# Attention batches of four tiles across head groups, with the engine of the k and q evacuations chosen by position

## The chip, the cores and the metric

One NeuronCore of one Trainium2 chip runs the whole program. The metric is the device time of one execution in microseconds (us), median of several. The profile's span is that time without about 1.8 us around it. PE is TensorE's matmul stream, PEld its weight loads, DVE is VectorE, ACT is ScalarE, POOL is GpSimd, SP the engine that issues the DMAs; SPq and the like are the issuing side of an engine. TensorE writes into PSUM, a memory of eight banks; an *evacuation* is the copy by which ScalarE or VectorE takes a finished result out of a bank, so that the bank can be written again.

## The reference

Two attention blocks read the same x (2048 rows, 1024 columns, 32 heads of 32) and are mixed by a gate. A is linear attention; B, in which the change lies, lets each query see 8 keys at distances 0, 2, ..., 14.

```python
x = A_x
g = sigmoid((x * gate_w).sum(-1, keepdims=True))
a = A_ref(x, A_wqkv, A_wo)     # phi(q) (phi(k)^T v) / (phi(q) sum phi(k)), then @ wo
b = B_ref(x, B_wqkv, B_wo)     # softmax over 8 keys at distance 0, 2, ... 14, then @ wo
return g * a + (1 - g) * b
```

## The kernel before

Rows are sorted by parity, so that the 8 keys of a query are neighbours. A *tile* is one head group (4 heads) and 112 queries (128 at the start of a parity) against 128 keys; a head group has 18 tiles, 8 head groups have 144. A *score batch* computes the scores of some tiles into four PSUM banks, one per head; ScalarE takes the exp, VectorE multiplies by the band mask; a *value batch* then multiplies by V. The batches of head group c-1 are strewn between the 64 wide matmuls (8 groups of 8) that project k and q of head group c. Positions count these matmuls. The code is shortened and put together from the kernel; the kernel itself has every line.

```python
CUTS4 = (0, 4, 8, 12, 15, 18)        # 5 batches per head group: 4, 4, 4, 3, 3 tiles
CUTS3 = (0, 3, 6, 9, 12, 15, 18)     # the last head group: 6 batches of 3
# k and q projection, one group of 8 matmuls:
    nc.tensor.matmul(st["pj"][:], lhsT=W[...], rhs=xT[:, kt, cols], ...)   # 128x512, two PSUM banks in turn
    if kt == KT - 1:
        if which == 0: nc.scalar.copy(out=kqt[:, 0, cols], in_=st["pj"][:])          # k: ScalarE
        else:          nc.vector.tensor_copy(out=kqt[:, 1, cols], in_=st["pj"][:])   # q: VectorE
# scores(g), one score batch:
    s4 = ps_s.tile([P, 4, 512], F32, ...)                    # four banks, not doubled
    for q0, w, k0 in tiles:
        for i in range(4):                                   # four heads: four 32-row tiles of the array
            r = slice(32 * i, 32 * i + 32)
            nc.tensor.matmul(s4[:, i, o:o + w], lhsT=kqt[r, 0, k0:k0 + P], rhs=kqt[r, 1, q0:q0 + w], ...)
        o += w
    for h in range(2):                                       # exp and mask, two heads at a time
        nc.scalar.activation(out=ptv[:, hs], in_=s4[:, hs, 0:W_], func=ACT.Exp, scale=SCALE)
        nc.vector.tensor_tensor(out=ptv[:, hs], in0=ptv[:, hs], in1=mask..., op=ALU.mult)
# pv(g), one value batch, 17 matmuls later: 128-row matmuls of 33 columns (V and a column of ones),
# then reciprocal and product on VectorE, then a DMA transpose (all cut)
ev.append((first + step * g, scores)); ev.append((first + step * g + lag, pv))   # step = 64 / batches
```

Of the kernel before, what the change touches and what calls it, by code (L numbers as in the profile page):

```python
# [7 lines left out]
ACT = mybir.ActivationFunctionType  # L8
ALU = mybir.AluOpType
BF16 = mybir.dt.bfloat16  # L10
F32 = mybir.dt.float32
PE = mybir.EngineType.PE
DVE = mybir.EngineType.DVE
P = 128
# [14 lines left out]
def interleave(units, events):  # L29

    events = sorted(events, key=lambda e: e[0])
    for i, unit in enumerate(units):
        while events and events[0][0] <= i:
            events.pop(0)[1]()
        unit()
    for _, fn in events:
        fn()
# [3 lines left out]
def kernel(  # L41
# [11 lines left out]
    nc = tc.nc  # L53
    S, D = A_x.shape[1:]
# [9 lines left out]
    Dh = D // H  # L64
# [1 line left out]
    NB = S // P  # L66
    SCALE = float(Dh) ** -0.5
    QT = query_tiles()
    CUTS4 = (0, 4, 8, 12, 15, 18)
    CUTS3 = (0, 3, 6, 9, 12, 15, 18)  # L70

    nc.scalar.preload_act_table_set("natural_log_exp_and_others")

    consts = ctx.enter_context(tc.tile_pool(name="consts", bufs=1))
# [48 lines left out]
    def band(dst, lead):  # L123
        nc.gpsimd.memset(dst, 1.0)
        for base, sign in ((lead, 1), (7 - lead, -1)):
            nc.gpsimd.affine_select(out=dst, in_=dst, compare_op=ALU.is_ge, fill=0.0, base=base,
                                    pattern=[[sign, dst.shape[1]]], channel_multiplier=-sign)

    mask = consts.tile([P, 128 + 5 * 112], BF16, name="mask")
    band(mask[:, 112:240], 0)  # L130
    for o in (0, 240, 352, 464, 576):
        band(mask[:, o:o + 112], 16)
    gdot = consts.tile([P, NB], F32, name="gdot")
    ratio = consts.tile([P, NB], F32, name="ratio")
# [13 lines left out]
    with tc.manual_schedule(engines={PE}):  # L148
# [172 lines left out]
        with ExitStack() as s2:  # L321
# [10 lines left out]
            def kq_units(c, kqt):  # L332
                def mm(b, which, kt, st):
                    W = (WkB, WqB)[which]
                    cols = slice(b * 512, (b + 1) * 512)
                    if kt == 0:
                        st["pj"] = ps_pj.tile([P, 512], F32, name="kq_ps", tag="pj")
                    nc.tensor.matmul(st["pj"][:], lhsT=W[c // 4][:, kt, (c % 4) * P:(c % 4 + 1) * P],  # L338
                                     rhs=xT[:, kt, cols], start=(kt == 0), stop=(kt == KT - 1))
                    if kt == KT - 1:  # L340
                        if which == 0:
                            nc.scalar.copy(out=kqt[:, 0, cols], in_=st["pj"][:])
                        else:
                            nc.vector.tensor_copy(out=kqt[:, 1, cols], in_=st["pj"][:])  # L344
                for b in range(4):
                    for which in range(2):
                        st = {}
                        for kt in range(KT):
                            yield lambda b=b, which=which, kt=kt, st=st: mm(b, which, kt, st)

            count = [0]

            def attention_events(c, kqt, cuts, first, lag):
                GROUPS = [QT[a:b] for a, b in zip(cuts, cuts[1:])]
                state = [dict() for _ in GROUPS]
                per_bank = 2 if cuts is CUTS4 else 3

                def scores(g):
                    tiles, st = GROUPS[g], state[g]
                    W_ = sum(w for _, w, _ in tiles)  # L360
                    s4 = ps_s.tile([P, 4, 512], F32, name="s4", tag="s")
                    o = 0
                    for q0, w, k0 in tiles:
                        for i in range(4):
                            r = slice(32 * i, 32 * i + 32)
                            nc.tensor.matmul(s4[:, i, o:o + w], lhsT=kqt[r, 0, k0:k0 + P],
                                             rhs=kqt[r, 1, q0:q0 + w], start=True, stop=True)
                        o += w
                    pt = PT[count[0] % 2]
                    count[0] += 1  # L370
                    ptv = pt[:, 0:4 * W_].rearrange("p (i s) -> p i s", i=4)
                    m0 = 112 if tiles[0][1] == 128 else 0 if tiles[1][1] == 128 else 240
                    for h in range(2):
                        hs = slice(2 * h, 2 * h + 2)
                        nc.scalar.activation(out=ptv[:, hs], in_=s4[:, hs, 0:W_], func=ACT.Exp, scale=SCALE)  # L375
                        m = mask[:, m0:m0 + W_]
                        nc.vector.tensor_tensor(out=ptv[:, hs], in0=ptv[:, hs],  # L377
                                                in1=m[:, None, :].broadcast_to([P, 2, W_]), op=ALU.mult)
                    st["pt"], st["W"] = pt, W_

                def pv(g):
                    tiles, st = GROUPS[g], state[g]
                    pt, W_, n = st["pt"], st["W"], len(tiles)
                    Ob = small.tile([P, 4, 4, Dh], BF16, name="Ob", tag="Ob", bufs=4)
                    oB = []
                    for b in range((n + per_bank - 1) // per_bank):
                        bank = ps_o.tile([P, 512], F32, name=f"oB{b}", tag=f"o{b}")
                        m = min(per_bank, n - per_bank * b)
                        oB.append((b * per_bank, m, bank[:, 0:m * 4 * (Dh + 1)].rearrange("p (t i e) -> p t i e", t=m, i=4)))
                    for t0, m, o_ in oB:  # L390
                        for i in range(4):
                            o = sum(w for _, w, _ in tiles[:t0])
                            for tt in range(t0, t0 + m):
                                nc.tensor.matmul(o_[:, tt - t0, i, :], lhsT=pt[:, i * W_ + o:i * W_ + o + P],
                                                 rhs=V[:, cuts[g] + tt, c * 4 + i, :], start=True, stop=True)
                                o += tiles[tt][1]
                    for t0, m, o_ in oB:
                        rd = small.tile([P, 3, 4, 1], F32, name="rd", tag="rd")
                        nc.vector.reciprocal(out=rd[:, 0:m], in_=o_[:, :, :, Dh:Dh + 1])
                        nc.vector.tensor_tensor(out=Ob[:, t0:t0 + m], in0=o_[:, :, :, 0:Dh],  # L400
                                                in1=rd[:, 0:m].broadcast_to([P, m, 4, Dh]), op=ALU.mult)
                    t0 = 0
                    while t0 < n:
                        q0, w, _ = tiles[t0]
                        m = 1
                        while t0 + m < n and tiles[t0 + m][1] == w and tiles[t0 + m][0] == q0 + m * w:
                            m += 1
                        nc.sync.dma_start_transpose(
                            out=OBT[:, c, q0:q0 + m * w].rearrange("p (t s) -> p t s", t=m),
                            in_=Ob[0:w, t0:t0 + m].rearrange("p t i e -> p (t i e)"))  # L410
                        t0 += m

                ev = []
                step = 64 / len(GROUPS)
                for g in range(len(GROUPS)):
                    ev.append((first + step * g, lambda g=g: scores(g)))
                    ev.append((first + step * g + lag, lambda g=g: pv(g)))
                return ev

            carry = []  # L420
            prev = None
            for c in range(KT):
                kqt = kq.tile([P, 2, S], BF16, name="kqt", tag="kq")
                ev = carry + (attention_events(c - 1, prev, CUTS4, 3, 17) if c else [])
                interleave(list(kq_units(c, kqt)), [e for e in ev if e[0] < 64])
                carry = [(p - 64, f) for p, f in ev if p >= 64]
                prev = kqt


            WoB = load_w("WoB", B_wo, 0, "wb")  # L430
# [38 lines left out]
                        for c in range(KT):  # L469
                            yield lambda c0=c0, n=n, side=side, c=c, st=st: mm(c0, n, side, c, st)  # L470

            turn = [0]

            def bank8():
                turn[0] += 1
                if turn[0] % 3 == 0:
                    return ps_o.tile([P, 512], F32, name="q_ps1", tag="o1")
                return ps_pj.tile([P, 512], F32, name="q_ps", tag="pj")

            ev = carry + attention_events(KT - 1, prev, CUTS3, 3, 17)  # L480
            interleave([u for t in range(12, 16) for u in qa_units(t, bank8, qa_keep)], [e for e in ev if e[0] < 64])
            carry = [(p - 64, f) for p, f in ev if p >= 64]
            interleave(list(out_units(0, bank8)), carry)
            pqT.append(big.tile([P, KT, 1536], BF16, name="pqT1", tag="vV"))
            for r0 in (512, 1024):
                nc.sync.dma_start_transpose(out=pqT[1][:, :, r0 - 512:r0], in_=pqd[r0:r0 + 512, :])
# [42 lines left out]
```

## Time and profile before

493.66 us, median of 3 runs (492.73 to 494.03).

| | before |
|---|---|
| span of the profiled run | 491.1 us |
| TensorE busy, VectorE, ScalarE | 98%, 58%, 37% |
| the stretch (below) | 161.84 us |
| score batches: of 4 tiles, of 3 tiles | 21, 20 |

From the page: busy time by engine (share of the span, x instructions), and the chain of work that ended last, by engine.

```profile
PE 481.1 (98%) x3276; PEld 230.0 (47%) x3336; DVE 282.8 (58%) x548; ACT 180.6 (37%) x279; POOL 7.6 (2%) x26
...
PE 91%; SPq 5%; DMA 2%; issue 1%; DVE 0%; ACT 0%; ACTq 0%
```

TensorE is the limit. What another engine saves counts only where TensorE would have waited for it. These are all the waits of PE (us in total, times, longest).

```profile
PE kq_ps L338 <- issue: 1.3, 8, 0.2
PE warm L163 <- DVE onesb L116: 1.1, 1, 1.1
PE pk_ps L157 <- DMA WkA_75<-in_A_wqkv_dram: 0.7, 1, 0.7
PE pk_ps L157 <- DMA xT<-in_A_x_dram: 0.4, 1, 0.4
PE pk_ps L157 <- DMA WkA_96<-in_A_wqkv_dram: 0.3, 1, 0.3
PE q_ps L295 <- issue: 0.3, 2, 0.2
```

All but the "issue" lines lie in the first 35 us. The "issue" gaps on L338 and L295 are not waits: each stands behind a score batch beside a wide matmul that the trace lost (7 of a group of 8 are recorded).

I call *the stretch* the time from the first k matmul to the first matmul of the second output tile: 608 wide matmuls with all attention batches between. The windows view gives, for the head of the kernel, the stretch and the tail: from and to, length, busy us (x instructions) of PE, PEld, DVE, ACT and POOL, then the granted TensorE clock (1.00 is full), the busy share of the DMA engines, and GB/s.

```profile
0.00:222.39 222.39, 218.66 (x1060) 103.10 (x1081) 153.03 (x239) 68.07 (x115) 7.56 (x26) 1.00 0.46 134
222.39:384.23 161.84, 159.07 (x1731) 78.50 (x1761) 104.28 (x274) 86.71 (x124) 0.00 (x0) 1.00 0.27 60
384.23:491.10 106.87, 103.33 (x488) 48.43 (x495) 25.47 (x36) 25.84 (x40) 0.00 (x0) 1.00 0.24 65
```

The timeline of PE inside the stretch (start us, duration us, what, count):

```profile
271.12 0.81 PE L338 MATMUL kq_ps<-xT,WkB_1039 128*128 128x512 bf16 x3
271.87 0.38 PE L366 MATMUL s_2538<-kqt 32*128 32x128 bf16 x16
272.18 1.25 PE L338 MATMUL kq_ps<-xT,WkB_1039 128*128 128x512 bf16 x5
```

Read starts, not durations: a wide matmul is listed with 0.379 us, but starts every 0.216 us. Here three of them start at 271.12, so the array is free at 271.77; the scores start at 271.87, 0.10 us later; they hold the array until 272.18, 0.31 us. So this batch of four tiles costs 0.41 us.

### The profile page before, as it was taken

Reading aid. Unit: us, or ns where it says so; the run is one execution under the profiler, and the core shown is the slowest. Engines: PE = TensorE matmul, PEld = TensorE weight load, DVE = VectorE, ACT = ScalarE, POOL = GpSimd, SP = SyncE. Lnnn points to the kernel's source line nnn. Section 1 sums busy time; section 2 is a strip of 40 time slices with the busy share of each in tenths; the row PEclk is TensorE's granted clock in tenths of the full one; section 3 lists DMA queues with packets and bytes.
Section 4 is the critical chain, followed back from the end, with each engine's and each line's share of the span. In section 5 each row is a group of like instructions: output and inputs, shape, how many; then the busy total and the mean of one; then the engine's idle time right before and its main releaser. Section 6 shows DMA issues by size and latency. Waiting matters only on the chain.

```text
span 491.1 us, 8153 instructions
## 1 busy us (share of the span) xinstructions
PE 481.1 (98%) x3276; PEld 230.0 (47%) x3336; DVE 282.8 (58%) x548; ACT 180.6 (37%) x279; POOL 7.6 (2%) x26
## 2 busy tenths in 40 slices
PE   8999999999999999999999999999999999999997
PEld 5444444446444444444445444444544444444444
DVE  1666669951329999997476767676765496000000
ACT  2333321112543333332555555655565333112121
POOL 3000000000200000000000000000000000000000
PEclk9999999999999999999999999999999999999999
DMA  8999950001521222235011133111174933010101
GB/s 195 173 297 368 348 183 0 0 1 44 177 76 54 86 94 92 73 135 173 4 34 30 32 96 54 26 36 37 29 136 90 217 87 84 35 43 33 43 34 43
DMA packets 80309, 46.56 MB, mean 95 GB/s; under 512 B 53648, under 2 KB 74256, under 8 KB 80272
## 3 DMA queue, kind: packets, MB, share of 16 engines
q1 hardware_dynamic: 80272, 46.04, 34.4%
q8 instruction: 26, 0.43, 0.4%
q14 instruction: 11, 0.09, 0.1%
HBM read 21.23 MB, written 7.34 MB: 58 GB/s over the span
## 4 chain that ended last, share of the span: by engine, by line
PE 91%; SPq 5%; DMA 2%; issue 1%; DVE 0%; ACT 0%; ACTq 0%
PE kq_ps L338 23%; PE d_ps L457 21%; PE g_ps L202 11%; PE p_ps L261 11%; PE p_ps L295 8%; PE pk_ps L157 6%; SPq L104 4%; PE q_ps L295 2%; DMA WkA_96<-in_A_wqkv_dram 2%; PE kv_ps L220 1%; PE q_ps_4355 L457 1%; PE p_ps L250 1%; PE q_ps L457 1%; SPq L101 0%; PE q_ps_4236 L295 0%
## 5 line engine op out<-in xcount | busy, mean ns | idle before, releaser
L202 PE MATMUL g_ps<-pk,xrow 128*128 128x512 bf16 x251 | 55.2, 379 | 0.3
L145 DVE TENSOR_SCALAR e<-e 128x512 f32<-128x512 f32 x64 | 27.2, 425 | 42.7 <-ACT e L144 42.7
L462 ACT ACTIVATE osb<-d_ps,omg 128x512 bf16<-128x512 f32 (+1 forms) x31 | 20.9, 673 | 74.5 <-PE d_ps L457 68.7
L157 PEld LDWEIGHTS <-xT 128*128 128x128 bf16 x256 | 24.9, 98 | 32.5 <-issue 1.5
L457 PEld LDWEIGHTS <-OBT 128*128 128x128 bf16 x264 | 25.8, 98 | 29.2
L202 PEld LDWEIGHTS <-xrow 128*128 128x128 bf16 x256 | 25.0, 98 | 30.2
L261 PEld LDWEIGHTS <-xT 128*128 128x128 bf16 x256 | 25.0, 98 | 30.2
L295 PEld LDWEIGHTS <-xT 128*128 128x128 bf16 x256 | 24.2, 98 | 28.0
L144 ACT ACTIVATE e<-pk_ps 128x512 f32<-128x512 f32 x32 | 19.0, 597 | 42.3 <-PE pk_ps L157 33.2
L377 DVE TENSOR_TENSOR PT_1863<-PT_1863,mask 128x672 bf16<-128x672 bf16 (+3 forms) x42 | 23.7, 571 | 17.9 <-ACT PT_1863 L375 17.4
L338 PE MATMUL kq_ps<-xT,WqB_1846 128*128 128x512 bf16 x120 | 31.8, 379 | 1.0 <-issue 0.6
L338 PE MATMUL kq_ps<-xT,WqB_1844 128*128 128x512 bf16 x124 | 31.7, 379 | 0.7 <-issue 0.5
L377 DVE TENSOR_TENSOR PT_1864<-PT_1864,mask 128x672 bf16<-128x672 bf16 (+3 forms) x40 | 22.3, 565 | 17.0 <-ACT PT_1864 L375 16.5
L338 PE MATMUL kq_ps<-xT,WkB_1041 128*128 128x512 bf16 x122 | 31.6, 379 | 0.2
L344 DVE CAST kqt<-kq_ps 128x512 bf16<-128x512 f32 x32 | 22.0, 687 | 16.5 <-PE kq_ps L338 16.5
L338 PE MATMUL kq_ps<-xT,WkB_1039 128*128 128x512 bf16 x120 | 30.7, 379 | 0.4 <-issue 0.2
L261 PE MATMUL p_ps<-WvB_112,xT 128*128 128x512 bf16 x126 | 30.6, 379 | 0.1
L261 PE MATMUL p_ps<-WvB_110,xT 128*128 128x512 bf16 x125 | 30.6, 379 | 0.1
L266 ACT CAST tmp<-p_ps 128x512 bf16<-128x512 f32 x32 | 18.8, 588 | 30.2 <-PE p_ps L261 27.9
L457 PEld LDWEIGHTS <-pqT_4413 128*128 128x128 bf16 x200 | 19.6, 98 | 22.1
L157 PE MATMUL pk_ps<-WkA_75,xT 128*128 128x512 bf16 x125 | 28.1, 380 | 1.4 <-DMA WkA_75<-in_A_wqkv_dram 0.7
L457 PE MATMUL d_ps<-WoB_4050,OBT 128*128 128x512 bf16 (+1 forms) x126 | 28.3, 365 | 0.1
(393 smaller groups left out, 665.8 us busy)
## 6 DMA issues: line engine op xcount, KB each, us to landing
xrow<-in_A_x_dram SPq DMA_DIRECT2D x4, 1024.0 KB, 13.0
out_dram<-osb SPq DMA_DIRECT2D x31, 128.0 KB, 1.9
pqd<-tmp SPq DMA_DIRECT2D x12, 256.0 KB, 2.0
V<-tmp SPq DMA_DIRECT2D x4, 264.0 KB, 2.4
WkA_75<-in_A_wqkv_dram SPq DMA_DIRECT2D x4, 256.0 KB, 3.8
WkA_96<-in_A_wqkv_dram SPq DMA_DIRECT2D x1, 1024.0 KB, 8.5
WvA_102<-in_A_wqkv_dram SPq DMA_DIRECT2D x1, 1024.0 KB, 15.3
WvA_104<-in_A_wqkv_dram SPq DMA_DIRECT2D x1, 1024.0 KB, 14.7
```

Of the source, the lines that this page charges most:

```text
L104: nc.sync.dma_start_transpose(out=xT[:, :, t * P:(t + 1) * P], in_=rows(x, t * P, (t + 1) * P))
L144: nc.scalar.activation(out=e[:], in_=pj[:], func=ACT.Exp)
L145: nc.vector.tensor_scalar(out=e[:], in0=e[:], scalar1=1.0, scalar2=1e-6, op0=ALU.min, op1=ALU.add)
L157: nc.tensor.matmul(pj[:], lhsT=xT[:, kt, t * P:(t + 1) * P], rhs=WkA[half][:, kt, :], start=(kt == 0), stop=(kt == KT - 1))
L202: nc.tensor.matmul(pj[:], lhsT=xrow[:, t, kt * P:(kt + 1) * P], rhs=pk[:, t, half * 512:(half + 1) * 512], start=(t == 0), stop=(t == NB - 1))
L261: nc.tensor.matmul(st["pj"][:], lhsT=xT[:, kt, t * P:(t + 1) * P], rhs=WvB[half][:, kt, :], start=(kt == 0), stop=(kt == KT - 1))
L295: nc.tensor.matmul(st["pj"][:], lhsT=xT[:, kt, t * P:(t + 1) * P], rhs=WqA[half][:, kt, :], start=(kt == 0), stop=(kt == KT - 1))
L338: nc.tensor.matmul(st["pj"][:], lhsT=W[c // 4][:, kt, (c % 4) * P:(c % 4 + 1) * P], rhs=xT[:, kt, cols], start=(kt == 0), stop=(kt == KT - 1))
L344: nc.vector.tensor_copy(out=kqt[:, 1, cols], in_=st["pj"][:])
L377: nc.vector.tensor_tensor(out=ptv[:, hs], in0=ptv[:, hs], in1=m[:, None, :].broadcast_to([P, 2, W_]), op=ALU.mult)
L457: nc.tensor.matmul(st["ps"][:, 0:n], lhsT=lhsT, rhs=W[c0 // 512][:, c, c0 % 512:c0 % 512 + n], start=(side == 0 and c == 0), stop=(side == ...
L462: nc.scalar.activation(out=osb[:, 0:n], in_=st["ps"][:, 0:n], func=ACT.Copy, scale=omg[:, tb:tb + 1])
```

## The change

The 144 tiles become one run of 36 batches of four, evenly spaced, some of them with tiles of two head groups. An evacuation of k or q goes to VectorE if its group ends within 4 matmuls behind a score batch (ScalarE is then in the exps), and to ScalarE otherwise: 16 on VectorE and 48 on ScalarE, as against 32 and 32. The q projection of A and the first output tile, which run beside the last attention batches, no longer borrow a third bank. A value batch now stands 18 matmuls behind its scores, not 17. The diff, cut to its core:

```diff
-                        if which == 0:
-                            nc.scalar.copy(out=kqt[:, 0, cols], in_=st["pj"][:])
-                        else:
-                            nc.vector.tensor_copy(out=kqt[:, 1, cols], in_=st["pj"][:])
+                        after = (64 * c + 16 * b + 8 * which + 8 - 67) % (512 / 36)
+                        (nc.vector.tensor_copy if 0 <= after < 4 else nc.scalar.copy)(
+                            out=kqt[:, which, cols], in_=st["pj"][:])
...
-                GROUPS = [QT[a:b] for a, b in zip(cuts, cuts[1:])]
+            TILES = [(c, t) for c in range(KT) for t in range(18)]
+            state = [dict() for _ in range(len(TILES) // 4)]
...
+                p_ = 64 + 3 + 512 * g / len(state)
+                events.append((p_, lambda g=g: scores(g)))
+                events.append((p_ + 18, lambda g=g: pv(g)))
...
-                if turn[0] % 3 == 0:
-                    return ps_o.tile([P, 512], F32, name="q_ps1", tag="o1")
                 return ps_pj.tile([P, 512], F32, name="q_ps", tag="pj")
```

(Cut: the mask, widened for the new places of the 128-wide tile; the rewritten loops of scores and values, whose work per tile is the same; the calls.)

More of the change, by code (lines that the diff above doesn't have):

```diff
@@ L68 @@
     QT = query_tiles()
-    CUTS4 = (0, 4, 8, 12, 15, 18)
-    CUTS3 = (0, 3, 6, 9, 12, 15, 18)
     nc.scalar.preload_act_table_set("natural_log_exp_and_others")
@@ L127, in band @@
                                     pattern=[[sign, dst.shape[1]]], channel_multiplier=-sign)
-    mask = consts.tile([P, 128 + 5 * 112], BF16, name="mask")
-    band(mask[:, 112:240], 0)
-    for o in (0, 240, 352, 464, 576):
+    mask = consts.tile([P, 128 + 7 * 112], BF16, name="mask")
+    band(mask[:, 336:464], 0)
+    for o in (0, 112, 224, 464, 576, 688, 800):
         band(mask[:, o:o + 112], 16)
@@ L349, in kq_units @@
                             yield lambda b=b, which=which, kt=kt, st=st: mm(b, which, kt, st)
-            count = [0]
-            def attention_events(c, kqt, cuts, first, lag):
-                GROUPS = [QT[a:b] for a, b in zip(cuts, cuts[1:])]
-                state = [dict() for _ in GROUPS]
-                per_bank = 2 if cuts is CUTS4 else 3
-                def scores(g):
-                    tiles, st = GROUPS[g], state[g]
-                    W_ = sum(w for _, w, _ in tiles)
-                    s4 = ps_s.tile([P, 4, 512], F32, name="s4", tag="s")
-                    o = 0
-                    for q0, w, k0 in tiles:
-                        for i in range(4):
-                            r = slice(32 * i, 32 * i + 32)
-                            nc.tensor.matmul(s4[:, i, o:o + w], lhsT=kqt[r, 0, k0:k0 + P],
-                                             rhs=kqt[r, 1, q0:q0 + w], start=True, stop=True)
-                        o += w
-                    pt = PT[count[0] % 2]
-                    count[0] += 1
-                    ptv = pt[:, 0:4 * W_].rearrange("p (i s) -> p i s", i=4)
-                    m0 = 112 if tiles[0][1] == 128 else 0 if tiles[1][1] == 128 else 240
-                    for h in range(2):
-                        hs = slice(2 * h, 2 * h + 2)
-                        nc.scalar.activation(out=ptv[:, hs], in_=s4[:, hs, 0:W_], func=ACT.Exp, scale=SCALE)
-                        m = mask[:, m0:m0 + W_]
-                        nc.vector.tensor_tensor(out=ptv[:, hs], in0=ptv[:, hs],
-                                                in1=m[:, None, :].broadcast_to([P, 2, W_]), op=ALU.mult)
-                    st["pt"], st["W"] = pt, W_
-                def pv(g):
-                    tiles, st = GROUPS[g], state[g]
-                    pt, W_, n = st["pt"], st["W"], len(tiles)
-                    Ob = small.tile([P, 4, 4, Dh], BF16, name="Ob", tag="Ob", bufs=4)
-                    oB = []
-                    for b in range((n + per_bank - 1) // per_bank):
-                        bank = ps_o.tile([P, 512], F32, name=f"oB{b}", tag=f"o{b}")
-                        m = min(per_bank, n - per_bank * b)
-                        oB.append((b * per_bank, m, bank[:, 0:m * 4 * (Dh + 1)].rearrange("p (t i e) -> p t i e", t=m, i=4)))
-                    for t0, m, o_ in oB:
-                        for i in range(4):
-                            o = sum(w for _, w, _ in tiles[:t0])
-                            for tt in range(t0, t0 + m):
-                                nc.tensor.matmul(o_[:, tt - t0, i, :], lhsT=pt[:, i * W_ + o:i * W_ + o + P],
-                                                 rhs=V[:, cuts[g] + tt, c * 4 + i, :], start=True, stop=True)
-                                o += tiles[tt][1]
-                    for t0, m, o_ in oB:
-                        rd = small.tile([P, 3, 4, 1], F32, name="rd", tag="rd")
-                        nc.vector.reciprocal(out=rd[:, 0:m], in_=o_[:, :, :, Dh:Dh + 1])
-                        nc.vector.tensor_tensor(out=Ob[:, t0:t0 + m], in0=o_[:, :, :, 0:Dh],
-                                                in1=rd[:, 0:m].broadcast_to([P, m, 4, Dh]), op=ALU.mult)
-                    t0 = 0
-                    while t0 < n:
-                        q0, w, _ = tiles[t0]
-                        m = 1
-                        while t0 + m < n and tiles[t0 + m][1] == w and tiles[t0 + m][0] == q0 + m * w:
-                            m += 1
-                        nc.sync.dma_start_transpose(
-                            out=OBT[:, c, q0:q0 + m * w].rearrange("p (t s) -> p t s", t=m),
-                            in_=Ob[0:w, t0:t0 + m].rearrange("p t i e -> p (t i e)"))
-                        t0 += m
-                ev = []
-                step = 64 / len(GROUPS)
-                for g in range(len(GROUPS)):
-                    ev.append((first + step * g, lambda g=g: scores(g)))
-                    ev.append((first + step * g + lag, lambda g=g: pv(g)))
-                return ev
@@ L420 @@
-            carry = []
-            prev = None
-            for c in range(KT):
-                kqt = kq.tile([P, 2, S], BF16, name="kqt", tag="kq")
-                ev = carry + (attention_events(c - 1, prev, CUTS4, 3, 17) if c else [])
-                interleave(list(kq_units(c, kqt)), [e for e in ev if e[0] < 64])
-                carry = [(p - 64, f) for p, f in ev if p >= 64]
-                prev = kqt
+            kqts = {}
+            TILES = [(c, t) for c in range(KT) for t in range(18)]
@@ new lines, with scores @@
+            state = [dict() for _ in range(len(TILES) // 4)]
+            def scores(g):
+                st = state[g]
+                tiles = [(c, t, *QT[t]) for c, t in TILES[4 * g:4 * g + 4]]
+                W_ = sum(w for _, _, _, w, _ in tiles)
+                s4 = ps_s.tile([P, 4, 512], F32, name="s4", tag="s")
+                o = 0
+                for c, t, q0, w, k0 in tiles:
+                    for i in range(4):
+                        r = slice(32 * i, 32 * i + 32)
+                        nc.tensor.matmul(s4[:, i, o:o + w], lhsT=kqts[c][r, 0, k0:k0 + P],
+                                         rhs=kqts[c][r, 1, q0:q0 + w], start=True, stop=True)
+                    o += w
+                pt = PT[g % 2]
+                ptv = pt[:, 0:4 * W_].rearrange("p (i s) -> p i s", i=4)
+                firsts = [j for j in range(4) if tiles[j][3] == 128]
+                m0 = 112 * (3 - firsts[0]) if firsts else 464
+                m = mask[:, m0:m0 + W_]
+                for h in range(2):
+                    hs = slice(2 * h, 2 * h + 2)
+                    nc.scalar.activation(out=ptv[:, hs], in_=s4[:, hs, 0:W_], func=ACT.Exp, scale=SCALE)
+                    nc.vector.tensor_tensor(out=ptv[:, hs], in0=ptv[:, hs],
+                                            in1=m[:, None, :].broadcast_to([P, 2, W_]), op=ALU.mult)
+                st["pt"], st["W"], st["tiles"] = pt, W_, tiles
@@ new lines, in pv @@
+            def pv(g):
+                pt, W_, tiles = state[g]["pt"], state[g]["W"], state[g]["tiles"]
+                Ob = small.tile([P, 4, 4, Dh], BF16, name="Ob", tag="Ob", bufs=4)
+                oB = [ps_o.tile([P, 512], F32, name=f"oB{b}", tag=f"o{b}")[:, 0:2 * 4 * (Dh + 1)]
+                      .rearrange("p (t i e) -> p t i e", t=2, i=4) for b in range(2)]
+                for b in range(2):
+                    for i in range(4):
+                        o = sum(tl[3] for tl in tiles[:2 * b])
+                        for tt in range(2 * b, 2 * b + 2):
+                            c, t = tiles[tt][:2]
+                            nc.tensor.matmul(oB[b][:, tt - 2 * b, i, :], lhsT=pt[:, i * W_ + o:i * W_ + o + P],
+                                             rhs=V[:, t, c * 4 + i, :], start=True, stop=True)
+                            o += tiles[tt][3]
+                for b in range(2):
+                    rd = small.tile([P, 2, 4, 1], F32, name="rd", tag="rd")
+                    nc.vector.reciprocal(out=rd[:], in_=oB[b][:, :, :, Dh:Dh + 1])
+                    nc.vector.tensor_tensor(out=Ob[:, 2 * b:2 * b + 2], in0=oB[b][:, :, :, 0:Dh],
+                                            in1=rd[:].broadcast_to([P, 2, 4, Dh]), op=ALU.mult)
+                t0 = 0
+                while t0 < 4:
+                    c, _, q0, w, _ = tiles[t0]
+                    m = 1
+                    while t0 + m < 4 and tiles[t0 + m][0] == c and tiles[t0 + m][3] == w and \
+                            tiles[t0 + m][2] == q0 + m * w:
+                        m += 1
+                    nc.sync.dma_start_transpose(
+                        out=OBT[:, c, q0:q0 + m * w].rearrange("p (t s) -> p t s", t=m),
+                        in_=Ob[0:w, t0:t0 + m].rearrange("p t i e -> p (t i e)"))
+                    t0 += m
@@ new lines, with between @@
+            events = []
+            for g in range(len(state)):
+                p_ = 64 + 3 + 512 * g / len(state)
+                events.append((p_, lambda g=g: scores(g)))
+                events.append((p_ + 18, lambda g=g: pv(g)))
+            def between(a, b):
+                return [(p_ - a, f) for p_, f in events if a <= p_ < b]
+            for c in range(KT):
+                kqts[c] = kq.tile([P, 2, S], BF16, name="kqt", tag="kq")
+                interleave(list(kq_units(c, kqts[c])), between(64 * c, 64 * c + 64))
@@ L470, in out_units, with bank2 @@
                             yield lambda c0=c0, n=n, side=side, c=c, st=st: mm(c0, n, side, c, st)
-            turn = [0]
-            def bank8():
-                turn[0] += 1
-                if turn[0] % 3 == 0:
-                    return ps_o.tile([P, 512], F32, name="q_ps1", tag="o1")
+            def bank2():
                 return ps_pj.tile([P, 512], F32, name="q_ps", tag="pj")
-            ev = carry + attention_events(KT - 1, prev, CUTS3, 3, 17)
-            interleave([u for t in range(12, 16) for u in qa_units(t, bank8, qa_keep)], [e for e in ev if e[0] < 64])
-            carry = [(p - 64, f) for p, f in ev if p >= 64]
-            interleave(list(out_units(0, bank8)), carry)
+            interleave([u for t in range(12, 16) for u in qa_units(t, bank2, qa_keep)], between(512, 576))
+            interleave(list(out_units(0, bank2)), between(576, 700))
             pqT.append(big.tile([P, KT, 1536], BF16, name="pqT1", tag="vV"))
```

## The prediction

> **What bounds the kernel now.** TensorE does. The page's busy row gives PE 98% of a 491.1 us span, its chain of waits gives PE 91%, and the waits of PE name only 4.1 us of idle time, nearly all of it at the start. Its "issue" gaps (1.3 us, 8 times) sit beside missing matmul records. VectorE (58%) and ScalarE (37%) have slack.
>
> The change touches the stretch from 222.2 us to 384.2 us of the timeline: 162.0 us, 608 wide matmuls (512 of k and q, 96 behind them), with 144 attention tiles between. A run of 8 wide matmuls takes 1.728 us, so 0.216 us each (the Trainium skill, "TensorE: Matmul & The Clock Gate", section "Phases on the wall clock", has about 216 ns for this width; the trace agrees). 608 x 0.216 = 131.3 us leaves 30.7 us for attention. From the timeline of PE, start to start, less the wide matmuls:
> - scores of 4 tiles: 0.09 us gap ahead + 0.31 = 0.40 us; of 3 tiles: 0.09 + 0.26 = 0.35 us. So about 0.2 us is paid per batch, whatever its size. The skill ("TensorEngine Tiling (Array Packing)", "Key Properties") says that a change of tiling mode drains the engine; only scores use 32-row tiles. The trace agrees: the weight loads pause for 0.42 us before every score batch.
> - values of 4 tiles: 0.43 us; of 3 tiles: 0.325 us: proportional to tiles.
>
> Check: before has 21 batches of 4 and 20 of 3: 21 x 0.83 + 20 x 0.675 = 30.9 us, as against 30.7. So there is no hidden stall.
>
> **What the change does.** 41 batches become 36, all of 4 tiles. Matmuls, columns and transposed bytes stay. On PE: 36 x 0.83 = 29.9 us, so **1.0 us less, all on the critical path**.
>
> On the other engines: ten exps (0.11 us fixed each, from 928 against 672 columns) and ten mask products (0.17 us) go; k and q evacuations go from 32 on ScalarE and 32 on VectorE to 48 and 16 (0.59 and 0.69 us each). In that stretch ScalarE, 86.7 us, rises by about 8; VectorE, 104.4 us, falls by about 14. PE waited for neither before, so that buys nothing by itself; it keeps evacuations from queueing behind both exps (1.78 us), which would exceed the next group's 1.73 us. I expect no stalls in the k and q part.
>
> **Where it may cost.** In the q part of A (behind the eighth group) the third bank is gone and all evacuations stay on ScalarE. One group there ends just behind a score batch; counted out with the durations above, PE waits some 0.25 us once. Net gain: 0.8 to 1.0 us.
>
> **Time.** 493.66 - 1.0 = **492.6 us, range 491.3 to 493.9** (8 in 10; the runs before spread by 1.3 us). Faster by over 2%: 0.01; within 2%: 0.975; slower by over 2%: 0.015.
>
> **What would show it.** The same stretch takes about 161.0 us; 36 score batches, none with a PE wait ahead of it; score and value batches of 0.40 and 0.43 us start to start; the waits of PE still under 5 us; 16 evacuations on VectorE and 48 on ScalarE; all outside the stretch the same to 0.3 us.
>
> **What would make it wrong.** (1) A queue order on ScalarE or VectorE that puts an evacuation or a mask product behind something that waits, so that PE stalls once per batch: 36 x 0.3 us would be 10 us slower. (2) Stalls of before hidden in modelled busy times; then the gain is larger. (3) Batches that mix two head groups costing more in weight loads. (4) A lower granted clock.

## The result and the profile after

492.58 us, median of 6 runs (491.57 to 493.80); the kernel before, over 6 runs, 493.70 us. The ratio is 0.9982, 95% interval 0.9962 to 1.0001. A ratio here is the mean time of one kernel's fast runs over that of the other's of the same rounds, so it is not quite the ratio of the medians quoted. The verdict is "same": a gain of 0.2%, at the edge of what whole-kernel times can show.

The page of the changed kernel:

```profile
PE 483.8 (99%) x3336; PEld 229.7 (47%) x3336; DVE 271.5 (55%) x514; ACT 189.2 (39%) x285; POOL 8.8 (2%) x32
...
PE 98%; DMA 1%; SPq 0%; ACT 0%; issue 0%; ACTq 0%
```

Its PE busy time is *higher* because this trace lost no matmul (3336 against 3276 recorded). Nor does the chain speak of the change: that of before goes back into DMAs at a wait of 0.3 us for a load at 34.92 us, and among the other traces e1, which lost no record, has PE 92%, and e5, which lost 63, PE 97%. The waits of PE, complete:

```profile
PE pk_ps L155 <- DMA WkA<-in_A_wqkv_dram: 1.5, 2, 1.3
PE warm L161 <- DVE onesb L113: 1.1, 1, 1.1
PE pk_ps L155 <- DMA xT<-in_A_x_dram: 1.0, 1, 1.0
```

The "issue" gaps are gone with the lost records. The windows view for head, stretch and tail:

```profile
0.00:222.88 222.88, 219.19 (x1081) 102.51 (x1081) 153.07 (x239) 67.98 (x115) 8.76 (x32) 1.00 0.47 134
222.88:383.65 160.77, 160.77 (x1762) 78.77 (x1761) 92.85 (x240) 95.39 (x130) 0.00 (x0) 1.00 0.28 63
383.65:490.70 107.05, 103.80 (x497) 48.43 (x495) 25.57 (x36) 25.84 (x40) 0.00 (x0) 1.00 0.24 62
```

The stretch is 161.84 - 160.77 = **1.07 us** shorter. The spans differ by only 0.4 us, since in this pair the head took 0.49 us longer (DMA waits of 2.5 us in place of 1.4) and the tail 0.18 us. A batch costs what it did:

```profile
271.30 0.81 PE L336 MATMUL kq_ps<-xT,WkB 128*128 128x512 bf16 x3
272.04 0.38 PE L362 MATMUL s<-kqt 32*128 32x128 bf16 x16
272.36 1.04 PE L336 MATMUL kq_ps<-xT,WkB 128*128 128x512 bf16 x4
```

Gap 0.09 us, scores 0.32 us. From the unrounded starts, all 36 batches have a gap of 0.095 or 0.096 us and hold the array for 0.307 to 0.315 us, so those with tiles of two head groups cost no more (the prediction's third risk). The weight loads show a pause in front of each batch (form and count, busy us and mean ns, then idle time before them), first before, then after:

```profile
L366 PEld LDWEIGHTS <-kqt 32*128 32x128 bf16 x576 | 8.0, 92 | 17.4 <-issue 13.6 <-PE kq_ps L338 2.5 <-remote 0.4
L362 PEld LDWEIGHTS <-kqt 32*128 32x128 bf16 x576 | 7.9, 92 | 15.3 <-issue 15.3
```

All of it stands before the first load of a batch: 17.4 us in 41 batches and 15.3 us in 36 are 0.42 us each. Not all of it is lost to the matmul stream; what is lost is the subject of the experiments.

### The profile page after: what moved, and what is told of

The parts are those of the page before. It is cut to its first block, busy times and chain, and to the rows that moved or that the text cites. A ratio compares the mean times of both kernels' runs of the same rounds, so it can differ in the third digit from the quotient of the medians.

```text
span 490.7 us, 8152 instructions
## 1 busy us (share of the span) xinstructions
PE 483.8 (99%) x3336; PEld 229.7 (47%) x3336; DVE 271.5 (55%) x514; ACT 189.2 (39%) x285; POOL 8.8 (2%) x32
## 4 chain that ended last, share of the span: by engine, by line
PE 98%; DMA 1%; SPq 0%; ACT 0%; issue 0%; ACTq 0%
PE kq_ps L336 23%; PE d_ps L449 21%; PE p_ps L259 11%; PE g_ps L200 11%; PE pk_ps L155 11%; PE p_ps L293 8%; PE q_ps L293 3%; PE oB L387 3%; PE s L362 2%; PE q_ps L449 1%; DMA xT<-in_A_x_dram 1%; PE kv_ps L218 1%; PE p_ps L248 1%; SPq L94 0%; SPq L98 0%; PE z_ps L225 0%
## 5 line engine op out<-in xcount | busy, mean ns | idle before, releaser
L372 ACT ACTIVATE PT<-s 128x896 bf16<-128x896 f32 (+1 forms) x72 | 63.0, 926 | 24.5 <-PE s L362 24.5
L336 PE MATMUL kq_ps<-xT,WkB 128*128 128x512 bf16 x256 | 65.3, 379 | 0.0
L336 PE MATMUL kq_ps<-xT,WqB 128*128 128x512 bf16 x256 | 64.8, 379 | 0.0
L373 DVE TENSOR_TENSOR PT<-PT,mask 128x896 bf16<-128x896 bf16 (+1 forms) x72 | 44.6, 624 | 26.6 <-ACT PT L372 26.6
L155 PE MATMUL pk_ps<-WkA,xT 128*128 128x512 bf16 x256 | 56.1, 379 | 2.6 <-DMA WkA<-in_A_wqkv_dram 1.5
L259 PE MATMUL p_ps<-WvB,xT 128*128 128x512 bf16 x256 | 58.5, 379 | 0.0
L449 PE MATMUL d_ps<-WoA,pqT 128*128 128x512 bf16 (+1 forms) x248 | 56.9, 372 | 0.0
L449 PE MATMUL d_ps<-WoB,OBT 128*128 128x512 bf16 (+1 forms) x248 | 56.9, 372 | 0.0
L293 PE MATMUL p_ps<-WqA,xT 128*128 128x512 bf16 x192 | 43.4, 379 | 0.0
L341 ACT CAST kqt<-kq_ps 128x512 bf16<-128x512 f32 x48 | 28.2, 587 | 31.8 <-PE kq_ps L336 31.6
```

Source lines behind the costliest of these rows:

```text
L155: nc.tensor.matmul(pj[:], lhsT=xT[:, kt, t * P:(t + 1) * P], rhs=WkA[half][:, kt, :], start=(kt == 0), stop=(kt == KT - 1))
L259: nc.tensor.matmul(st["pj"][:], lhsT=xT[:, kt, t * P:(t + 1) * P], rhs=WvB[half][:, kt, :], start=(kt == 0), stop=(kt == KT - 1))
L293: nc.tensor.matmul(st["pj"][:], lhsT=xT[:, kt, t * P:(t + 1) * P], rhs=WqA[half][:, kt, :], start=(kt == 0), stop=(kt == KT - 1))
L336: nc.tensor.matmul(st["pj"][:], lhsT=W[c // 4][:, kt, (c % 4) * P:(c % 4 + 1) * P], rhs=xT[:, kt, cols], start=(kt == 0), stop=(kt == KT - 1))
L341: (nc.vector.tensor_copy if 0 <= after < 4 else nc.scalar.copy)(out=kqt[:, which, cols], in_=st["pj"][:])
L449: nc.tensor.matmul(st["ps"][:, 0:n], lhsT=lhsT, rhs=W[c0 // 512][:, c, c0 % 512:c0 % 512 + n], start=(side == 0 and c == 0), stop=(side == ...
```

## The experiments

The stretch, read from the trace, repeats to 0.01 us (161.84, 161.84 and 161.83 in the three traces with the old batches; 160.77 in all five with the 36 new ones and the rule), while whole-kernel runs of one kernel spread by 2 us. e5 to e8 are a single profiled execution each (state unknown).

| run | score batches | k and q evacuations | stretch, us |
|---|---|---|---|
| before | 41 | 32 ScalarE, 32 VectorE | 161.84 |
| after | 36 | rule (48, 16) | 160.77 |
| e1 | 36 | 32, 32 | 161.17 |
| e2 | 41 | rule (40, 24) | 161.84 |
| e3 | 36 | all ScalarE | 160.81 |
| e5 | 48 | rule | 163.36 |
| e6 | 72 | all ScalarE | 169.60 |
| e7, full rows | 36 | rule | 174.58 |
| e8, full rows | 48 | rule | 174.50 |

Theory: each score batch costs TensorE some 0.2 us beyond its work, and the change removes five. Rivals: the choice of engine brought the gain; or the end of the run did (third bank, six small batches); or it is noise.

### e1: the batches alone

```diff
-(nc.vector.tensor_copy if 0 <= after < 4 else nc.scalar.copy)(
+(nc.scalar.copy if which == 0 else nc.vector.tensor_copy)(
     out=kqt[:, which, cols], in_=st["pj"][:])
```

> The changed kernel with the old choice of engine: k always on ScalarE, q always on VectorE, 36 batches. Theory (the gain is the fixed cost of five score batches; the choice of engine only guards against stalls): the stretch from the first k matmul to the first matmul of the second output tile loses the same 1.07 us of batches, but some q evacuations now stand behind mask products and reciprocals on VectorE. Counted out with the durations of the trace, three of them make TensorE wait some 0.65 us each and a few 0.05 us, about 2 us in all: stretch about 162.9 us, whole kernel about 1 us slower than before. Rival A (the choice of engine gives nothing, batches alone do it): stretch 160.8 us and no waits of TensorE. Rival B (the choice of engine is what gave the gain): stretch 161.8 us or more without visible waits.

Measured: 161.17 us; ratio 0.9993 (0.9971 to 1.0015). The batches alone bring 0.67 us, and 0.40 us of their gain is given back. Set side by side batch by batch, the two traces part in three steps of 0.12 to 0.14 us, ahead of the batches that start 37.6, 72.6 and 107.7 us into the stretch of the changed kernel. Three is the number that was counted out; the size was put at 0.65 us each, five times too much, so the 162.9 us expected were missed by 1.7 us. The first step, in the timeline of e1:

```profile
258.56 1.89 PE L336 MATMUL kq_ps<-xT,WkB 128*128 128x512 bf16 x8
...
259.60 0.20 DVE L392 RECIPROCAL rd<-oB 128x8 f32<-128x8 f32 x1
259.72 0.64 DVE L341 CAST kqt<-kq_ps 128x512 bf16<-128x512 f32 x1
...
260.41 0.38 PE L336 MATMUL kq_ps<-xT,WqB 128*128 128x512 bf16 x1
```

Eight matmuls from 258.56 would let the next start at 260.29; it starts at 260.41, just behind the q evacuation, which VectorE began only at 259.72, in its queue behind a product, a mask product and a reciprocal, and ended at 260.36. In the changed kernel ScalarE has that evacuation, and the eight take 1.73 us:

```profile
258.47 1.89 PE L336 MATMUL kq_ps<-xT,WkB 128*128 128x512 bf16 x8
258.71 0.59 ACT L341 CAST kqt<-kq_ps 128x512 bf16<-128x512 f32 x1
...
260.20 0.38 PE L336 MATMUL kq_ps<-xT,WqB 128*128 128x512 bf16 x1
```

Two lessons. The engine matters once the batches move, though it gains nothing by itself (e2). And a wait of PE under some 0.16 us (0.379 us listed less 0.216 us of spacing) leaves no gap: e1's list of waits names nothing in the stretch, and the windows view calls PE busy all through it. Only starts against starts show it.

```profile
222.97:384.14 161.17, 161.17 (x1761) 78.78 (x1760) 102.10 (x256) 86.22 (x114) 0.00 (x0) 1.00 0.27 63
```

### e2: the rule alone

```diff
 # in the kernel before, 41 batches
+after = (16 * b + 8 * which + 8 - 3) % (64 / 5)
+(nc.vector.tensor_copy if 0 <= after < 4 else nc.scalar.copy)(out=kqt[:, which, cols], in_=st["pj"][:])
```

> The kernel before with its 41 batches, but k and q evacuated on VectorE where the group ends within 4 matmuls behind a score batch, else on ScalarE. Theory: TensorE waited for nothing in that stretch before, so nothing changes: stretch 161.8 us, ratio 1.000. Rival B (the choice of engine gave the gain): stretch about 160.8 us, ratio 0.998.

Measured: stretch 161.84 us, every batch within 0.01 us of its place in the kernel before.

```profile
223.91:385.75 161.84, 161.84 (x1762) 78.53 (x1760) 99.70 (x266) 92.15 (x132) 0.00 (x0) 1.00 0.27 60
```

The rule alone gains nothing, so the first rival falls (with these positions it puts 40 evacuations on ScalarE and 24 on VectorE). The whole-kernel ratio, though, was 0.9972 with an interval of 0.9949 to 0.9996: by that number alone one would have called it faster. What stands behind that is in e4 and e9.

### e3: every evacuation on ScalarE

```diff
-(nc.vector.tensor_copy if 0 <= after < 4 else nc.scalar.copy)(
-    out=kqt[:, which, cols], in_=st["pj"][:])
+nc.scalar.copy(out=kqt[:, which, cols], in_=st["pj"][:])
```

> The changed kernel with every k and q evacuation on ScalarE. Theory with durations counted out: an evacuation behind both exps (1.6 us) ends just as its bank is needed, since a value batch stands in the next group and stretches it to 2.15 us; so TensorE waits at most some 0.2 us in all: stretch 160.8 to 161.1 us. The reading given for the rule in the prediction (an evacuation behind both exps takes longer than the next group) expects waits of 0.3 to 0.5 us in each of the 8 groups that end soonest behind a score batch, some 3 to 4 us: stretch 164 us.

Measured: 160.81 us (ratio 0.9981, 0.9959 to 1.0003). An evacuation behind both exps is hardly ever late, so the rule's second branch is worth 0.04 us. Of the 0.40 us that the rule is worth, 0.36 us comes from taking q off VectorE (161.17 to 160.81).

### e4: the changed kernel again, five rounds

> The changed kernel itself in five rounds, for a narrower interval. Theory: 1.07 us of 493.7 us less, ratio 0.9978, with the interval below 1. If the difference seen so far is noise of the head of the kernel: an interval that holds 1.

Measured: stretch 160.77 us again; 492.28 us as against 494.36 us, ratio 0.9970 (0.9951 to 0.9988). The interval is below 1, but the 0.3% are too good. Each run lists its mean granted clock: of the 11 runs of before in this job, 8 have 0.996 or 0.997 and took 494.09 to 494.76 us, and 3 have 1.0 and took 492.45 to 493.12 us. Of the 6 changed ones a single run has 0.997 (493.50 us); the others took 491.56 to 492.95. So two modes, some 1.5 us apart, fell unevenly on the two kernels. All of these count as fast runs. The profiled run of e4 is one of the low mode; its windows (last three figures: granted clock, DMA share, GB/s) show where:

```profile
6.00:8.00 2.00, 0.99 (x4) 0.19 (x2) 0.00 (x0) 0.00 (x0) 0.00 (x0) 0.92 1.08 166
8.00:10.00 2.00, 1.68 (x4) 0.58 (x5) 0.00 (x0) 0.00 (x0) 0.00 (x0) 0.50 1.16 315
10.00:12.00 2.00, 2.00 (x8) 0.84 (x7) 0.00 (x0) 0.00 (x0) 0.00 (x0) 0.73 1.02 207
```

The clock is at half just behind the waits for the first loads, long before the changed code. The three rows lack 2.00 x (0.08 + 0.50 + 0.27) = 1.7 us of full clock, so it was at half for 3.4 us; the wide matmuls of this trace start every 0.427 us there in place of 0.216. The clock record gives 3.41 us in each of the five traces of the low mode (e2, e3, e4, e6, e11). One thing sets these apart: in the 3.41 us ahead of the dip PE was busy for only 1.47 to 1.73 us. In the nine traces without a dip, in the first 3.41 us after the clock rose, it was busy for 1.80 (e1) to 3.41 us (e9). For e4 and the profiled run of after:

```profile
4.27:7.68 3.41, 1.70 (x13) 0.69 (x10) 0.00 (x0) 0.00 (x0) 1.50 (x8) 1.00 1.08 237
3.77:7.18 3.41, 1.91 (x17) 0.95 (x15) 0.00 (x0) 0.00 (x0) 1.97 (x10) 1.00 1.07 233
```

This order of 14 traces was found afterwards; no run was made to test where the limit lies.

### e5 and e6: batches of three and of two

```diff
-TILES[4 * g:4 * g + 4]
+TILES[N * g:N * g + N]        # N = 3: 48 batches; N = 2: 72 (value batches 12 matmuls later, all on ScalarE)
```

> The changed kernel with 48 batches of three tiles in place of 36 of four. Theory (a fixed cost per score batch; from 161.84 us with 41 batches and 160.77 us with 36, 0.214 us each): stretch 160.77 + 12 x 0.214 = 163.3 us. Rival (the gain came from the end of the run, that is the third bank, the six batches of three in the last head group or the earlier last value batch): stretch about 160.8 us, as long as TensorE shows no waits.

> The changed kernel with 72 batches of two tiles, all k and q evacuations on ScalarE, value batches 12 matmuls behind their scores (18 would need a third buffer). Theory: stretch 160.77 + 36 x 0.214 = 168.5 us, on a straight line with 36, 41 and 48 batches. Rival: no line in the number of batches.

Measured: 163.36 us with 48 batches (expected 163.3), with no waits listed in the stretch but "issue" gaps as in before. With 72: 169.60 us (expected 168.5), of which 0.8 us is one listed wait of a value batch for VectorE; the other 0.3 us is not accounted for. Per batch, from 36: 0.214 us (41), 0.216 us (48), 0.245 us (72; 0.223 without the wait). The time follows the number of batches.

```profile
222.08:385.44 163.36, 159.72 (x1728) 78.17 (x1760) 102.09 (x312) 96.34 (x154) 0.00 (x0) 1.00 0.28 61
223.93:393.53 169.60, 165.82 (x1730) 76.58 (x1760) 103.81 (x296) 110.42 (x218) 0.00 (x0) 1.00 0.26 55
```

Starts against starts say the same: a batch of 2, 3 or 4 tiles holds the array for 0.21, 0.26 or 0.31 us, 0.05 per tile and 0.11 besides, and with the gap of 0.095 us that makes 0.206 us per batch. And e5 has the changed kernel's banks and end, so the second rival falls.

### e7 and e8: the same batches without a change of tiling mode

```diff
-lhsT=kqts[c][r, 0, k0:k0 + P], rhs=kqts[c][r, 1, q0:q0 + w]     # r: 32 rows of head i
+lhsT=kqts[c][:, 0, k0:k0 + P], rhs=kqts[c][:, 1, q0:q0 + w]     # all 128 rows
```

> Wrong result on purpose: the score matmuls of the changed kernel take all 128 rows (the four heads of a group summed) in place of 32-row tiles, so the tiling mode never changes. 36 batches of four tiles. The 64 matmuls of 128 columns in the kv step took 3.57 us, 0.056 us each, which makes about 0.050 us for these of 114 columns, 0.79 us per batch. If the fixed 0.2 us is the price of changing the mode: it goes, stretch 160.77 + 36 x (0.79 - 0.40) = 175 us. If it is paid for any score batch (waits for the four banks, for k and q, for exps): stretch about 182 us.

> Wrong result on purpose: as the run before, but 48 batches of three tiles. If the fixed cost is the change of mode: the same stretch as with 36 full-row batches, within 0.5 us. If it is paid per batch whatever the mode: 12 x 0.214 = 2.6 us longer than with 36.

The results are wrong (only the sizes and order of the work count; both passed the comparison, presumably since with this data the scores are too small to move the softmax beyond its tolerance). Measured: 174.58 us with 36 batches (expected 175) and 174.50 us with 48 (expected within 0.5 us of each other).

```profile
222.01:396.59 174.58, 172.87 (x1730) 102.61 (x1760) 93.62 (x240) 95.34 (x130) 0.00 (x0) 1.00 0.26 58
222.21:396.71 174.50, 172.56 (x1727) 102.57 (x1760) 101.46 (x312) 97.86 (x154) 0.00 (x0) 1.00 0.26 57
```

Twelve more batches cost nothing here, where they cost 163.36 - 160.77 = 2.59 us with 32-row tiles. The value batches are 12 more as well, so they carry no fixed cost either. So the 0.214 us is the price of going into 32-row tiles and back, not of a batch as such. Why it has this size was not tested. The loads give a hint: in e1 the first score load and its matmul both start at 256.76, while the load of a wide group starts at 258.35, 0.21 us ahead of its matmul; with full rows, in e7, the scores have that lead too (252.96 and 253.18). The groups view of PEld for the scores of e7, then of e8, shows that the pause of 0.42 us is gone: the idle time is 0.12 us at most before any one load, as between wide matmuls, and no single gap is long enough for the view to name what ended it.

```profile
L362 PEld LDWEIGHTS <-kqt 128*128 128x128 bf16 x576 | 32.2, 98 | 8.5
```

```profile
L363 PEld LDWEIGHTS <-kqt 128*128 128x128 bf16 x576 | 33.3, 98 | 11.4
```

### e9, e10 and e11: the head filled, before and after

The head runs 36 small matmuls on ones (`warm_up`) until the first loads are there; these runs put 20 more into the waits.

```diff
-warm_up(36)
+warm_up(44)                                    # 128x128 matmuls on ones
 for kt in kts:                                 # first two row tiles of the first projection
     project(first[t], t, kt, 0)
+    # and warm_up(2) behind the second matmul of tile 0, warm_up(10) ahead of tile 1
```

> The kernel before with its idle head filled: 44 warm-up matmuls in place of 36, two more between the second and third projection matmul and ten more ahead of the second row tile, all in time in which TensorE waits for the first loads. Runs with a mean granted clock of 0.996 or 0.997 took 494.1 to 494.8 us, runs of the same kernel at 1.0 took 492.5 to 493.1; in the trace of such a run the clock is at half from 7.8 to 10.5 us, just behind those waits. Theory: the spread of the whole-kernel times comes from this head, so a filled head shows clock 1.0 in all or nearly all runs, about 492.6 us median, ratio 0.997 to the unfilled one, and less spread. If the dip has another cause: the same mixture of clocks, ratio 1.000.

> The changed kernel with the same filled head. Theory: 1.07 us below the run before with the filled head, about 491.5 us median, faster than both kernels (ratio 0.995 to the kernel before), stretch 160.77 us. If the stretch is not what the whole time follows: no difference between the two filled ones.

> The changed kernel a third time, as the partner of the filled one on the same chip and in the same rounds. Theory: runs at clock 1.0 take about 492.2 us, those at 0.997 about 493.6; ratio to the kernel before 0.998 if both have the same share of dips, lower if the kernel before has more.

Measured: with a filled head, no run of 11 was in the low mode (clock 0.999 or 1.0 in all); in the same job 3 of 11 runs of before and 1 of 6 of the changed kernel were. So it is consistent with a filled head keeping the mode away. (The dip is longer than was expected above: in e4 it lasts from 7.68 to 11.10 us by the clock record.) The stretches are 161.83 and 160.77 us. The medians: 492.97 us (before, filled), 492.39 us (after, filled), 492.50 us (after). The ratios to the kernel before are 1.0001 (0.9984 to 1.0017), 0.9987 (0.9970 to 1.0003) and 0.9983 (0.9966 to 1.0000). The gain expected of the fill (ratio 0.997 and 0.995) did not come. In this job few runs were in the low mode, so there was little to win; and at clock 0.999 or 1.0 the filled kernels took longer in the mean than the unfilled ones, by 0.48 us (before) and 0.16 us (after), which is not explained.

The two filled kernels differ by 0.70 us in the mean, not 1.07; runs at clock 0.999 or 1.0 of this job by 0.38 us (before 492.65, 8 runs; after 492.27, 5 runs). Some of the gain is lost outside the stretch. Part of that is in the traces: from the end of the last evacuation to the end of the span they show 2.52 to 2.54 us in three traces shaped like before (before, e2, e9) and 2.73 to 2.75 us in six shaped like the changed kernel (after, e3, e4, e7, e10, e11). That takes 0.2 of the 1.07 us back.

### e12: four more transposes

The changed kernel issues 60 transposes of the attention output, the kernel before 64, so its last stores stand four places on in the rotation of eight DMA semaphores.

```diff
-... and tiles[t0 + m][2] == q0 + m * w:
+... and tiles[t0 + m][2] == q0 + m * w and not (g in (0, 1, 3, 5) and t0 + m == 2):   # split four of them
```

> The changed kernel with the filled head and four of its transposes of the attention output split in two, 64 in place of 60 as in the kernel before, so that the last stores to the output use the same places of the eight rotating DMA semaphores as there. From the end of the last evacuation to the end of the span the three traces of kernels shaped like the one before took 2.49 to 2.54 us, the traces of the changed one 2.69 to 2.77. Theory (the place in the rotation sets that end): 2.5 us, so 0.25 us back, about 492.1 us median, and the fastest of all by a little. If the end has another cause: 2.7 us or more, and about 492.4 us as with 60. The stretch stays at 160.77 us in both.

Measured: 492.21 us (492.01 to 492.60), and the kernel before in the same job 493.51 us; ratio 0.9974 (0.9952 to 0.9995); the end takes 490.25 - 487.72 = 2.53 us. That agrees with the theory, and so does e6 (2.50 us), but it is not settled: e5 and e8 put their last stores on the same places and took 3.0 us, and e1, with the places of the changed kernel, took 3.3. It is the lowest ratio among the versions with a filled head, but one run of before in this job took 496.23 us (clock 0.993); by the runs at clock 0.999 or 1.0 the two differ by 1.10 us. Of these nine runs of before, five took 493.47 to 494.53 us at clock 1.0, so the dip is not the only source of spread. The 0.2 to 0.3 us by which e12 leads e10 and e11 are within the spread between jobs.

## Why the prediction was right

- **TensorE bounds the stretch, without hidden waits.** Right: e2 changed two engines' queues and moved nothing.
- **1.0 us less, all on the critical path.** Measured 1.07 us. The sum was 36 x 0.83 against 21 x 0.83 + 20 x 0.675; the fixed part, put at about 0.2 us, is 0.214 us by the count of batches.
- **The fixed part is the drain on a change of tiling mode.** The prediction leaned on the skill's word and the pause of the weight loads. e7 and e8 show that the cost comes with the 32-row tiles and goes with them; that a drain is what takes the time stays the skill's word.
- **The rule buys nothing by itself, it guards.** Right in e2, and e1 shows the guarded loss, 0.40 us. But the reason given (an evacuation behind both exps is too late) is wrong: e3 puts all of them on ScalarE and loses 0.04 us. It is VectorE's queue that made q late.
- **0.25 us of waiting in the q part.** Did not come. There, in the trace, the evacuation ended at 371.42 + 0.59 = 372.01 us and the bank was due at 370.98 + 5 x 0.216 = 372.06 us. The term was mis-sized. The prediction reckons with the full records of two exps; here these are listed with 1.73 us together, while the next instruction of ScalarE began 1.61 us after the first exp did.
- **ScalarE up by about 8 us, VectorE down by about 14.** ScalarE rose by 8.7; VectorE fell by 11.4. It was off the critical path.
- **All outside the stretch the same to 0.3 us.** Wrong in the profiled pair: head 0.49 us longer, by DMA waits of the first loads. Other traces of the changed code have heads from 222.01 to 224.14 us, so this is mostly spread. The 0.2 us at the end repeated in six traces. The rest of what separates 1.07 us in the stretch from about 0.4 to 0.7 us in whole runs of e4 and of e9 to e11 is not settled.
- **492.6 us** was close to the measured 492.58, but such a match is luck at 0.05 us: two modes of the head, some 1.5 us apart, decide more.

## What to carry to other kernels

When one engine is 98% busy, price a rearrangement by starts to starts on that engine; here each trip into row-tiled matmuls cost 0.21 us, so fewer and fuller batches are worth just that times the number removed. When batches move, recheck who evacuates in their shadow: the same batches with the old engines gave back 0.40 of 1.07 us, in waits too short for the profile to list. And look at clock modes before trusting a ratio: a variant with an unchanged stretch measured 0.9972 with its interval below 1.

## What the Trainium skill lacked or had wrong

- "TensorEngine Tiling (Array Packing)", "Key Properties", says that a change of tiling mode drains the engine, but gives no cost. Here a trip from full rows into 32-row tiles and back costs the matmul stream 0.214 us, and the weight loads pause for 0.42 us; with full rows, 36 and 48 batches take the same time (174.58 and 174.50 us).
- "TensorE: Matmul & The Clock Gate", "Back-to-back issue gap", gives about 131 ns per matmul of 512 columns and 81 ns per matmul of 128 as sustained in real streams of weight load and matmul. Here such streams run at 216 ns (1.728 us for eight) and 56 ns (3.57 us for 64): the figures which that page has for the isolated case there and, in the section that the prediction cites, for back-to-back matmuls.
- The same page, "HAM oscillation — how this bites in real kernels", speaks of idle gaps over about 3.4 us. Here the clock fell to half for 3.41 us behind waits of at most 0.8 to 1.2 us each, in five traces whose PE was busy for 1.47 to 1.73 of the 3.41 us before; nine traces with 1.80 us and more kept the full clock, one of them with a wait of 1.3 us. By the mean clock (0.999 or 1.0) a filled head had no such dip in 17 runs (5 of e9, 6 of e10, 6 of e12).
- "Perfetto Trace Analysis", "Identifying the Most-Contended Engine", rightly warns of matmul busy time. No page says that waits under about 0.16 us vanish in it altogether: e1 lost 0.40 us with PE called busy for 161.17 of 161.17 us.
- No page tells what makes the time from the last evacuation to the end of a kernel's span vary. It took 2.50 to 3.33 us here with identical work behind it; one trace with the rotation of DMA semaphores shifted by four took 2.53 in place of 2.73 us.
